# A hand-ordered attention and MoE kernel: other orders for its five engines' instruction lists

## The chip, the cores and the metric

The kernel runs on one core of a Trainium2 chip. The core has five engines with an instruction stream each: TensorE (PE, with its weight loads shown as PEld), VectorE (DVE), ScalarE (ACT), GpSimd (POOL) and SyncE (SP). Each stream runs in order, and an instruction that waits holds back all that stand behind it on its engine. The metric is device microseconds of one execution; less is better. The times are medians of a few runs.

## What is computed

Causal attention over 8 batches of 8 heads (576 tokens of 64 values, 16 extra "beacon" keys and values that every token sees), then a two-layer MLP with a quick GELU on the 4608 tokens that come out:

```python
k_all = np.concatenate([beacon_k, k], axis=2)
v_all = np.concatenate([beacon_v, v], axis=2)
scores = scale * np.matmul(q, k_all.transpose(0, 1, 3, 2))
scores = np.where(causal, -1000000000.0, scores)
a = np.exp(scores - scores.max(-1, keepdims=True))
a /= a.sum(-1, keepdims=True) + 1e-09
x = np.matmul(a, v_all)            # (8, 8, 576, 64), then 4608 tokens x 512
h = x @ w_in                       # 512 -> 2048
g = h * (1.0 / (1.0 + np.exp(-1.702 * h)))
out = g @ w_out                    # 2048 -> 512
```

## The kernel before

**Tiling.** Attention is done in 16 sets: a set is four heads of one batch (`HS = 2` sets a batch). For each set, queries and keys are loaded by GpSimd's DMA queue (`e_load_qk`, L397), transposed on DVE (`e_turn`, L446, with the line of the transposes at L455), and multiplied on TensorE in chunks of at most 512 score columns a head (`e_qk`, L474; four row tiles of 32). The chunks are numbered through: qk0 to qk54. ACT takes the exponential of each chunk from PSUM (`e_exp`, L492). POOL, and DVE for the first two sets, put zeros in the masked corners (`e_mask`, L502). Then `e_av` (L565; column tiles of 32) multiplies with the values, or with ones for the sum of each row; DVE makes the reciprocal of the sums (`e_z1`, `e_z2`) and writes the product to the activations `xT` (`e_norm`). A visit named av5.0.1 is set 5, part 0, half 1.

The tokens go through the MLP in ten groups: two of 256 tokens, then eight of 512. m1.1.4 is the first layer (`e_m1`, L619) of group 1 for hidden tile 4. Groups 0 and 1 apply the activation as a tanh on ACT (`e_tanh`, L640) and a gate on DVE (`e_gate`, L660, its instruction at L663), the later ones as one gelu on ACT. m2.0.1.2 is the second layer of group 0, row half 1, third quarter of the hidden rows (`e_m2`). Groups 2 to 9 use Strassen-like products of 2x2 blocks for the second layer (`e_prod`, named m2.g.p.n) with joins on DVE, and groups 7 to 9 also for the first (`e_part`).

**What sets the order.** The kernel schedules by hand. Every step is recorded as an operation with a number, an engine, a price and the operations it depends on (`Plan.op`). The table `ORDER` lists, for each engine, the numbers in the order in which it issues them; "Q" lists the landings of POOL's loads, which are no instructions. `Plan.run` (L150) replays these lists with the prices, which gives each operation a planned start, and the steps are then written out in the order of planned starts (L1320). The replay also picks the PSUM bank for each visit that needs one: the bank that is free first. Four banks serve all visits but qk while attention runs; the scores of qk take the other four.

**Names that matter below.** Numbers in the lists: 129, 131, 134 are qk5, qk6, qk7; 152, 161, 158, 164, 167, 170, 173 are m1.0.0, m1.0.6, m1.0.4, m1.0.8, m1.0.10, m1.0.12, m1.0.14, and the number behind each of these is its tanh on ACT (165 for m1.0.8), the next one its gate on DVE. 188, 191, 194, 197, 203, 200 are m1.1.0, m1.1.2, m1.1.4, m1.1.6, m1.1.10, m1.1.8; their gates are 190, 193, 196, 199, 205, 202. On POOL, 53 and 55 load the keys and the queries of set 3, 57 and 59 the third and the fourth quarter of the second layer's weights w2 (`e_load_w2`, L426, 512 KB of 16-bit values each), 133, 137 and 136 are masks of set 1. On DVE, 255 casts set 3's beacon keys, 256 transposes its keys (a small transpose of the beacon keys is part of it) and 257 its queries. POOL has eight completion semaphores for loads; each load waits for the landing of the eighth before it. The first layer's weights w1 come in four column blocks, each in two loads (upper and lower half of the rows); m1.0.6 needs the second block.

Of the kernel before, what the change touches and what calls it, by code (L numbers as in the profile page):

```python
# [17 lines left out]
        76, 100, 115, 118, 120, 106, 138, 141, 143, 108, 155, 111, 152, 129, 161, 158, 122, 131, 164, 167, 134, 127,  # L18
        170, 173, 176, 145, 125, 148, 150, 177, 182, 188, 191, 227, 194, 197, 232, 183, 203, 234, 200, 178, 237, 179,
        206, 258, 241, 209, 184, 263, 185, 212, 265, 213, 248, 246, 268, 214, 215, 401, 251, 253, 272, 218, 404, 275,  # L20
        244, 279, 219, 220, 407, 282, 284, 277, 221, 414, 320, 296, 304, 290, 302, 292, 300, 298, 312, 308, 294, 318,
        314, 310, 306, 316, 426, 435, 423, 343, 338, 339, 340, 433, 431, 438, 344, 345, 359, 349, 341, 464, 346, 350,
        351, 352, 354, 574, 355, 429, 360, 361, 577, 356, 362, 357, 372, 365, 583, 474, 477, 373, 366, 374, 367, 605,
        480, 484, 375, 482, 607, 368, 506, 502, 488, 492, 610, 490, 486, 498, 504, 500, 508, 514, 510, 516, 494, 496,
        512, 534, 593, 596, 535, 536, 539, 540, 550, 541, 542, 537, 742, 545, 546, 547, 548, 603, 745, 551, 552, 553,
        599, 601, 619, 622, 748, 555, 556, 557, 558, 561, 755, 625, 627, 629, 562, 563, 776, 568, 564, 569, 570, 571,
        779, 764, 767, 659, 637, 641, 657, 649, 651, 647, 661, 635, 631, 653, 805, 772, 770, 774, 643, 655, 633, 639,
        645, 679, 680, 815, 818, 700, 681, 682, 684, 701, 915, 690, 685, 686, 691, 692, 702, 918, 687, 693, 695, 703,
        696, 924, 821, 823, 697, 698, 706, 946, 825, 707, 713, 708, 709, 948, 934, 937, 714, 715, 716, 827, 951, 944,
        940, 942, 853, 831, 833, 855, 857, 851, 843, 835, 837, 847, 839, 845, 829, 849, 841, 1083, 960, 963, 875,  # L30
        876, 880, 877, 878, 881, 882, 1086, 968, 966, 970, 883, 1089, 902, 909, 903, 886, 891, 1096, 887, 888, 889,
        892, 893, 1117, 904, 894, 905, 896, 897, 1120, 898, 899, 910, 911, 1105, 1108, 1146, 912, 976, 994, 996, 972,
        978, 1000, 1002, 992, 984, 990, 986, 988, 974, 980, 982, 998, 1168, 1111, 1115, 1159, 1113, 1156, 1025, 1026,
        1020, 1027, 1171, 1021, 1022, 1028, 1023, 1031, 1177, 1032, 1033, 1164, 1166, 1162, 1199, 1034, 1036, 1047,
        1048, 1037, 1201, 1041, 1042, 1038, 1039, 1233, 1049, 1204, 1043, 1044, 1050, 1235, 1237, 1054, 1055, 1056,
        1057, 1239, 1249, 1190, 1241, 1265, 1251, 1242, 1253, 1255, 1187, 1245, 1267, 1258, 1281, 1257, 1269, 1216,
        1195, 1197, 1193, 1213, 1261, 1271, 1285, 1287, 1283, 1273, 1289, 1274, 1219, 1221, 1223, 1334, 1290, 1293,
        1277, 1357, 1335, 1313, 1318, 1314, 1336, 1315, 1319, 1316, 1320, 1321, 1373, 1324, 1325, 1337, 1326, 1329,
# [9 lines left out]
        1, 3, 77, 79, 103, 101, 107, 109, 112, 153, 156, 130, 159, 162, 132, 165, 168, 135, 171, 174, 189, 192, 228,  # L48
        195, 198, 233, 235, 201, 204, 238, 180, 207, 259, 210, 264, 186, 266, 269, 216, 402, 405, 408, 222, 417, 415,
        297, 291, 303, 305, 301, 299, 293, 309, 321, 295, 319, 313, 315, 311, 307, 317, 436, 439, 342, 465, 468, 575,  # L50
        578, 584, 587, 606, 608, 503, 507, 489, 491, 493, 487, 499, 505, 509, 515, 517, 495, 501, 511, 497, 513, 611,
        538, 743, 746, 749, 756, 758, 777, 780, 660, 642, 638, 652, 658, 648, 650, 636, 632, 662, 654, 806, 644, 634,
        656, 640, 646, 809, 916, 683, 919, 928, 925, 947, 949, 952, 828, 832, 854, 856, 852, 858, 834, 838, 844, 840,
        836, 846, 830, 848, 850, 842, 1084, 879, 1087, 1090, 1099, 1097, 1118, 1121, 1147, 1150, 977, 995, 997, 973,
        979, 1001, 993, 985, 991, 989, 1003, 975, 981, 987, 983, 999, 1169, 1172, 1024, 1181, 1178, 1200, 1202, 1234,
        1205, 1236, 1238, 1240, 1250, 1252, 1244, 1266, 1254, 1256, 1268, 1248, 1246, 1264, 1270, 1260, 1282, 1262,
        1272, 1286, 1284, 1288, 1276, 1280, 1292, 1294, 1296, 1278, 1358, 1317, 1374, 1378, 1376, 1360, 1362, 1364,
# [5 lines left out]
        73, 74, 75, 97, 98, 99, 80, 81, 82, 78, 116, 105, 87, 104, 117, 102, 121, 119, 139, 140, 144, 142, 157, 154,  # L63
        123, 163, 160, 124, 224, 169, 128, 166, 172, 175, 146, 147, 126, 149, 151, 225, 226, 398, 190, 193, 196, 199,
        255, 256, 257, 202, 205, 286, 242, 411, 287, 211, 208, 243, 399, 249, 247, 400, 250, 412, 254, 252, 273, 245,
        274, 280, 276, 413, 281, 285, 283, 278, 289, 461, 288, 462, 419, 580, 420, 463, 326, 327, 328, 421, 322, 92,
        323, 324, 422, 427, 428, 424, 425, 325, 330, 334, 329, 335, 432, 336, 331, 434, 337, 332, 333, 470, 347, 582,
        353, 471, 581, 472, 430, 473, 358, 363, 475, 476, 478, 479, 481, 485, 739, 483, 369, 376, 370, 589, 752, 740,
        590, 615, 518, 753, 921, 519, 754, 526, 591, 527, 520, 528, 592, 529, 521, 741, 522, 597, 523, 594, 530, 595,
        598, 531, 802, 532, 524, 533, 616, 543, 525, 604, 549, 617, 618, 554, 600, 620, 602, 623, 624, 621, 559, 760,  # L70
        628, 761, 762, 626, 630, 565, 763, 566, 768, 572, 765, 811, 812, 766, 803, 804, 769, 773, 771, 671, 1080,
        775, 672, 813, 922, 663, 814, 664, 675, 667, 816, 673, 819, 668, 669, 817, 923, 665, 666, 820, 674, 676, 677,
        1093, 670, 688, 694, 678, 930, 822, 824, 699, 931, 826, 932, 933, 704, 710, 938, 939, 935, 936, 717, 711,
        945, 941, 943, 1081, 956, 957, 958, 871, 1082, 1094, 1095, 959, 872, 873, 1225, 867, 859, 961, 962, 964, 965,
        860, 863, 1174, 1143, 861, 874, 862, 868, 864, 967, 865, 971, 866, 969, 884, 869, 870, 1101, 1144, 890, 1145,
        1102, 895, 1226, 1103, 1104, 900, 906, 1109, 907, 1110, 913, 1106, 1107, 1152, 1153, 1227, 1176, 1175, 1154,
        1012, 1004, 1005, 1155, 1006, 1112, 1116, 1008, 1160, 1016, 1013, 1009, 1157, 1161, 1007, 1114, 1158, 1017,
        1010, 1011, 1014, 1029, 1018, 1183, 1165, 1163, 1019, 1229, 1015, 1230, 1035, 1228, 1231, 1167, 1184, 1040,
        1232, 1209, 1045, 1185, 1051, 1052, 1186, 1058, 1210, 1191, 1243, 1192, 1247, 1211, 1212, 1188, 1189, 1263,
        1259, 1217, 1196, 1198, 1194, 1214, 1215, 1297, 1218, 1275, 1291, 1220, 1279, 1295, 1298, 1222, 1301, 1302,  # L80
        1303, 1305, 1309, 1306, 1310, 1353, 1299, 1354, 1307, 1322, 1300, 1355, 1356, 1224, 1308, 1311, 1304, 1312,
# [3 lines left out]
        1557, 1555, 1558, 1559, 1546, 1547, 1551, 1560, 1552, 1570, 1548, 1556, 1576, 1581, 1592, 1586, 1593, 1599,  # L85
    ],
    "POOL": [
        8, 10, 12, 14, 16, 17, 19, 21, 23, 25, 27, 29, 31, 33, 35, 37, 39, 41, 43, 45, 47, 110, 49, 51, 113, 114, 53,
        55, 57, 59, 133, 61, 136, 137, 63, 65, 67, 69, 71, 378, 230, 231, 229, 380, 382, 384, 386, 236, 388, 390,
        392, 239, 240, 394, 396, 261, 260, 262, 441, 443, 270, 267, 271, 449, 451, 453, 455, 457, 459, 403, 406, 445,  # L90
        447, 416, 409, 410, 437, 418, 719, 721, 466, 467, 440, 585, 588, 579, 576, 586, 469, 727, 723, 725, 729, 731,
        733, 735, 737, 609, 782, 784, 612, 613, 614, 747, 751, 744, 750, 757, 790, 792, 794, 786, 788, 796, 798, 800,
        778, 759, 781, 1060, 1062, 807, 808, 917, 920, 926, 810, 927, 1068, 1070, 1072, 1074, 1066, 1064, 1076, 1078,
        954, 955, 929, 950, 953, 1125, 1123, 1088, 1085, 1131, 1133, 1135, 1137, 1139, 1141, 1091, 1129, 1127, 1098,
        1092, 1122, 1100, 1149, 1119, 1151, 1148, 1170, 1179, 1173, 1180, 1203, 1206, 1208, 1182, 1207,
    ],
    "Q": [
# [1260 lines left out]
```

## Time and profile before

| | us |
|---|---|
| median of 3 runs (lowest to highest) | 324.79 (324.67 to 325.13) |
| the profiled execution: its own time | 324.84 |
| its span, first to last instruction | 323.1 |
| mean granted TensorE clock | 0.992 |
| first qk visit starts | 8.27 |
| ACT: idle time ended by a qk visit | 40.9 in 38 waits |
| POOL: idle time ended by an exponential | 94.2 in 16 waits |
| PE: idle time ended by an exponential | 2.0 in 4 waits |
| DMA: POOL's loads, packets and volume | 47,552, 18.49 MB |

Busy time is the time in which an engine's instructions run, idle time the gap before an instruction, put down to what ended it. TensorE's matmuls overlap in the pipeline, so that a matmul of 256 columns is shown as 273 ns though the next starts 109 ns later: steps from start to start say what TensorE is worth, durations do not. A load's own time is short on POOL (some 0.55 us for queries or keys, 0.75 us for a quarter of w2); its landing is a mark of its own, microseconds later.

### The profile page before, as it was taken

How to read it: one execution, taken by the hardware profiler on the slowest of the kernel's cores; microseconds unless marked ns; L12 is line 12 of the kernel's file. 1: busy time of each engine (PE TensorE's matmuls, PEld its weight loads, DVE VectorE, ACT ScalarE, POOL GpSimd, SP SyncE). 2: the span in 40 equal slices, each digit the busy share in tenths (PEclk: the TensorE clock that was granted, in tenths of full speed). 3: DMA queues.
4: the chain of work that ended last, by engine and by line, in shares of the span. 5: the costliest groups of instructions: out<-in, count | busy, mean ns of one | idle time of the engine just before them, and what ended most of it. 6: DMA issues, size and time to landing. Idle time of an engine off the chain costs nothing. (4 is left out here: it accounts for less than half of the span.)

```text
span 323.1 us, 10371 instructions
## 1 busy us (share of the span) xinstructions
PE 312.2 (97%) x4508; PEld 230.0 (71%) x4508; DVE 261.7 (81%) x524; ACT 219.5 (68%) x272; POOL 113.4 (35%) x178
## 2 busy tenths in 40 slices
PE   7689999999999999999999999999999999999994
PEld 7467665644776467745878877646888888888884
DVE  4837798777987989976998889986999895585784
ACT  1676597677767686689767696768778735974830
POOL 8775478190328403871058208600221000000000
PEclk9899999999999999999999999999999999999998
DMA  7999999294423941396019908900111001101112
GB/s 124 163 200 208 206 185 184 54 97 85 123 70 66 185 73 34 53 183 89 2 36 134 189 3 80 176 28 2 37 34 65 4 32 34 67 2 36 65 67 97
DMA packets 58222, 28.85 MB, mean 89 GB/s; under 512 B 41280, under 2 KB 53568, under 8 KB 58176
## 3 DMA queue, kind: packets, MB, share of 16 engines
q0 software_dynamic: 47552, 18.49, 48.4%
q1 hardware_dynamic: 10560, 9.69, 9.3%
q8 instruction: 35, 0.57, 0.7%
q14 instruction: 11, 0.09, 0.1%
q10 hardware_dynamic: 64, 0.01, 0.0%
HBM read 37.22 MB, written 9.44 MB: 144 GB/s over the span
## 5 line engine op out<-in xcount | busy, mean ns | idle before, releaser
L495 ACT ACTIVATE E<-s 128x2048 f16<-128x2048 f32 (+5 forms) x66 | 98.9, 1515 | 41.4 <-PE s L484 40.9
L630 PE MATMUL u<-xT,w 128*128 128x256 f16 (+1 forms) x512 | 87.3, 326 | 0.6 <-ACT g L651 0.5
L516 POOL TENSOR_SCALAR_AFFINE_SELECT E<-E 128x512 f16<-128x512 f16 (+3 forms) x78 | 48.8, 658 | 107.5 <-ACT E L495 94.2
L630 PEld LDWEIGHTS <-w 128*128 128x128 f16 x512 | 49.0, 98 | 34.7 <-issue 1.9
L651 ACT ACTIVATE g<-u 128x512 f16<-128x512 f32 x80 | 43.2, 599 | 15.6 <-PE u L630 15.4
L744 PEld LDWEIGHTS <-g 128*128 128x128 f16 x512 | 48.5, 98 | 7.1 <-issue 0.3
L744 PE MATMUL u<-w,g 128*128 128x256 f16 x384 | 49.9, 273 | 0.0
L760 DVE SCALAR_TENSOR_TENSOR osb<-u,osb 128x512 f32<-128x512 f32 x56 | 37.6, 683 | 13.6 <-PE u L744 11.7
L484 PEld LDWEIGHTS <-kT 32*128 32x128 f16 x1376 | 25.6, 93 | 20.6 <-issue 12.1
L744 PEld LDWEIGHTS <-sA 128*128 128x128 f16 x384 | 36.3, 98 | 5.1 <-issue 0.3
L484 PE MATMUL s<-qT,kT 32*128 32x32 f16 (+20 forms) x1376 | 34.9, 230 | 3.9 <-ACT E L495 2.0
L859 ACT ACTIVATE g<-u 128x512 f16<-128x512 f32 x48 | 26.9, 602 | 12.4 <-PE u L831 6.8
L744 PE MATMUL u<-tB,sA 128*128 128x256 f16 x256 | 34.9, 273 | 0.1
L606 DVE TENSOR_TENSOR xT<-u,rz 128x352 f16<-128x352 f32 (+2 forms) x52 | 25.8, 518 | 7.4 <-PE u L571 7.1
L415 POOL DMA_DIRECT2D vb<-in_v_dram x32 | 27.4, 876 | 2.2 <-DMA qn<-in_q_dram 1.2
L571 PE MATMUL u<-E,vb 128*32 128x352 f16 (+8 forms) x928 | 27.9, 265 | 0.0
L534 DVE TENSOR_TENSOR zs<-zs,E 128x1344 f16<-128x1344 f16 (+2 forms) x36 | 22.6, 628 | 2.3 <-POOL E L516 1.6
L571 PEld LDWEIGHTS <-vb 128*32 128x32 f16 (+1 forms) x928 | 19.8, 97 | 5.5 <-issue 1.5
L455 DVE STREAM_TRANSPOSE kT<-kn 128x576 f32<-128x576 f32 x16 | 20.1, 1258 | 2.3 <-DMA kn<-in_k_dram 1.5
L831 PE MATMUL u<-xT,w 128*128 128x256 f16 x144 | 20.5, 273 | 0.0
L831 PEld LDWEIGHTS <-w 128*128 128x128 f16 x192 | 18.8, 98 | 2.2
L455 DVE STREAM_TRANSPOSE qT<-qn 128x576 f32<-128x576 f32 x16 | 19.9, 1241 | 0.1
(73 smaller groups left out, 397.5 us busy)
## 6 DMA issues: line engine op xcount, KB each, us to landing
out_dram<-osb SPq DMA_DIRECT2D x36, 256.0 KB, 2.3
kn<-in_k_dram POOLq DMA_DIRECT2D x16, 288.0 KB, 6.3
qn<-in_q_dram POOLq DMA_DIRECT2D x16, 288.0 KB, 6.8
vb<-in_v_dram POOLq DMA_DIRECT2D x24, 128.0 KB, 6.6
w<-in_moe_w_in_dram POOLq DMA_DIRECT2D x8, 256.0 KB, 9.6
w<-in_moe_w_out_dram POOLq DMA_DIRECT2D x4, 512.0 KB, 13.8
vb<-in_v_dram POOLq DMA_DIRECT2D x8, 112.0 KB, 5.0
vb<-in_v_dram POOLq DMA_DIRECT2D x8, 80.0 KB, 7.8
```

The costliest lines, as they stand in the source:

```text
L415: nc.gpsimd.dma_start(out=t[0 : hi - lo, j, h0:h1, :], in_=v[b, h0:h1, lo:hi, :].rearrange("h n d -> n h d"),)
L455: nc.vector.transpose(out=f32(dst.rearrange("p n e -> p (n e)")).rearrange("p (r t) -> p t r", t=TR), in_=f32(src[:, :]).rearrange("p (t c ...
L484: nc.tensor.matmul(sc[:, h, o : o + w], kT[s % NB2][r : r + 32, j * P : (j + 1) * P, d], qT[s % NB2][r : r + 32, a : a + w, d], start=(d = ...
L495: nc.scalar.activation(out=Es[s][:, :, c0:c1], in_=ss[i][:, :, o : o + c1 - c0], func=AFT.Exp, scale=0.125,)
L516: nc.gpsimd.affine_select(out=blk, in_=blk, compare_op=ALU.is_ge, fill=0.0, base=off + (Nb if j == 0 else 0), pattern=[[0, Q], [1, w]], ch ...
L571: nc.tensor.matmul(u[32 * h : 32 * h + 32, a:e], lhs, src[0:kw, h, col : col + e - a], start=first, stop=last,)
L630: nc.tensor.matmul(u[:, o + a - t0 : o + e - t0], w1t[:, kp, nt * P : (nt + 1) * P], xT[:, kp, a % XR : (e - 1) % XR + 1], start=(kp == 0) ...
L651: nc.scalar.activation(out=gts[g][:, n0:n1, 0:w], in_=rings[("m1", g, n0)][:, 0 : n * w].rearrange("p (n w) -> p n w", n=n), func=AFT.Gelu ...
L744: nc.tensor.matmul(u[:, HM * mt : HM * (mt + 1)], lhs[:, n, mt * P : (mt + 1) * P], rhs[:, n, :], start=(n == 0 and mt == 0), stop=(n == H ...
L760: nc.vector.scalar_tensor_tensor(out=osbs[(g, dst)][:, :], in0=rings[("p", g, p)][:, :], scalar=scale_of(g), in1=osbs[(g, src)][:, :], op0 ...
L831: nc.tensor.matmul(u[:, HM * n : HM * (n + 1)], lhs[x][:, (2 * i + n) * P : (2 * i + n + 1) * P], rhs[:, x, :], start=fresh and n == 0 and ...
L859: nc.scalar.activation(out=gts[g][:, n : n + 2, HM * h : HM * (h + 1)], in_=rings[src][:, :].rearrange("p (n w) -> p n w", n=2), func=AFT. ...
```

## The change

Only the lists in `ORDER` differ. No operation is added or taken away: each engine has the same numbers, 559 on PE, 260 on ACT, 465 on DVE, 171 on POOL. PE's list differs from its 14th place to its 432nd, ACT's from its 15th to its 203rd, DVE's from its 23rd to its 385th, POOL's from its 27th to its last. The lists of SP and Q are the same. Because the planned starts follow from the lists, visits also get other PSUM banks.

The beginning of each changed list:

```diff
     "PE": [
-        76, 100, 115, 118, 120, 106, 138, 141, 143, 108, 155, 111, 152, 129, 161, 158, 122, 131, 164, 167, 134, 127,
-        170, 173, 176, 145, 125, 148, 150, 177, 182, 188, 191, 227, 194, 197, 232, 183, 203, 234, 200, 178, 237, 179,
...
+        76, 100, 115, 118, 120, 106, 138, 141, 143, 108, 155, 111, 152, 161, 129, 158, 164, 131, 167, 170, 134, 122,
+        173, 176, 125, 127, 145, 150, 148, 182, 177, 188, 191, 227, 183, 194, 197, 232, 184, 203, 234, 200, 178, 237,
...
     "ACT": [
-        1, 3, 77, 79, 103, 101, 107, 109, 112, 153, 156, 130, 159, 162, 132, 165, 168, 135, 171, 174, 189, 192, 228,
...
+        1, 3, 77, 79, 103, 101, 107, 109, 112, 153, 156, 130, 159, 162, 165, 132, 168, 171, 135, 174, 189, 192, 228,
...
     "DVE": [
...
-        123, 163, 160, 124, 224, 169, 128, 166, 172, 175, 146, 147, 126, 149, 151, 225, 226, 398, 190, 193, 196, 199,
-        255, 256, 257, 202, 205, 286, 242, 411, 287, 211, 208, 243, 399, 249, 247, 400, 250, 412, 254, 252, 273, 245,
...
+        163, 160, 224, 166, 169, 172, 123, 124, 175, 255, 126, 128, 146, 147, 149, 151, 225, 226, 190, 193, 257, 256,
+        196, 199, 202, 286, 398, 205, 208, 242, 399, 211, 461, 243, 400, 413, 247, 249, 245, 411, 273, 250, 274, 254,
...
     "POOL": [
-        8, 10, 12, 14, 16, 17, 19, 21, 23, 25, 27, 29, 31, 33, 35, 37, 39, 41, 43, 45, 47, 110, 49, 51, 113, 114, 53,
-        55, 57, 59, 133, 61, 136, 137, 63, 65, 67, 69, 71, 378, 230, 231, 229, 380, 382, 384, 386, 236, 388, 390,
...
+        8, 10, 12, 14, 16, 17, 19, 21, 23, 25, 27, 29, 31, 33, 35, 37, 39, 41, 43, 45, 47, 110, 49, 51, 113, 114,
+        133, 53, 137, 136, 57, 55, 59, 65, 61, 69, 71, 63, 67, 378, 229, 231, 384, 380, 230, 390, 239, 382, 394, 396,
```

In the built program the same change on POOL reads, in instructions (a line with L516 is a mask, L399 a load of queries or keys, L428 a quarter of w2):

```diff
 L399 DMACopy qn_93<-in_q_dram 128x1152
 L516 TensorScalarAffineSelect E<-E 128x4x128
+L516 TensorScalarAffineSelect E<-E 128x4x80 x2
+L399 DMACopy kn_94<-in_k_dram 128x1152
 L516 TensorScalarAffineSelect E<-E 128x4x80
-L399 DMACopy kn_94<-in_k_dram 128x1152
+L516 TensorScalarAffineSelect E<-E 128x4x128
+L428 DMACopy w_81<-in_moe_w_out_dram 128x4x512
 L399 DMACopy qn_91<-in_q_dram 128x1152
-L428 DMACopy w_81<-in_moe_w_out_dram 128x4x512 x2
...
+L428 DMACopy w_81<-in_moe_w_out_dram 128x4x512
```

Set 3's queries are the load into `qn_91`; its keys go to `kn_94`.

## The prediction

> **What bounds the kernel now.** I read part 1 of the page first, then the busy time of each engine by stretches of 20 us, then the order of time on PE, DVE and POOL in the first 45 us.
>
> ```profile
> PE 312.2 (97%) x4508; PEld 230.0 (71%) x4508; DVE 261.7 (81%) x524; ACT 219.5 (68%) x272; POOL 113.4 (35%) x178
> ...
> 0.00:20.00 20.00, 14.86 (x291) 12.79 (x292) 12.17 (x33) 8.59 (x8) 16.15 (x30) 0.91 1.25 154
> 20.00:40.00 20.00, 19.11 (x347) 14.05 (x345) 13.51 (x27) 13.56 (x18) 10.54 (x17) 1.00 1.20 207
> 40.00:60.00 20.00, 19.95 (x398) 12.17 (x400) 17.17 (x29) 16.47 (x16) 14.02 (x24) 1.00 1.55 174
> ...
> 180.00:200.00 20.00, 20.00 (x295) 16.44 (x293) 18.60 (x40) 15.24 (x19) 5.01 (x7) 1.00 0.45 69
> ```
>
> The columns of the stretches are length, then busy us of PE, PEld, DVE, ACT, POOL, then clock, DMA share and GB/s. From 40 us on PE has no hole to speak of. The DMA share is over 1 in the first 60 us: there the loads are the scarce thing. Busy PE is not PE at its peak, so I took each TensorE visit's usual length from the starts of its matmuls (start of a visit to start of the next, lower quartile of its like) and added them in order: 302.6 us of pure work. I call a visit's start less the work ahead of it its lag. Before, the lag is 8.27 at qk0 (only filler ran earlier), 12.62 at m1.0.4 (22.52 us), 12.97 at qk8 (36.24), 13.20 at m1.1.10 (40.22), 13.53 at qk19 (64.88) and 16.16 at the last visit (318.46): only about 2.6 us of waits are left after 65 us. A reorder can win little there; it can lose anywhere.
>
> ```profile
> 23.65 0.55 POOL L399 DMA_DIRECT2D kn<-in_k_dram  x1
> 24.48 0.53 POOL L399 DMA_DIRECT2D qn<-in_q_dram  x1 [0.28 <-issue]
> 25.49 0.75 POOL L428 DMA_DIRECT2D w<-in_moe_w_out_dram  x1 [0.48 <-DMA w<-in_moe_w_in_dram]
> 26.77 0.75 POOL L428 DMA_DIRECT2D w<-in_moe_w_out_dram  x1 [0.53 <-DMA w<-in_moe_w_in_dram]
> ...
> 36.98 0.69 DVE L663 SCALAR_TENSOR_TENSOR g<-sig,u 128x512 f16<-128x512 f16 x1 [0.19 <-ACT sig L644]
> 39.35 1.28 DVE L663 SCALAR_TENSOR_TENSOR g<-sig,u 128x512 f16<-128x512 f16 x2 [1.68 <-ACT sig L644]
> 40.55 1.33 DVE L440 CAST bkn<-bkf 128x64 f16<-128x64 f32 x1
> 41.92 0.21 DVE L448 STREAM_TRANSPOSE kT<-bkn 128x32 f32<-128x32 f32 x1
> 42.17 1.26 DVE L455 STREAM_TRANSPOSE kT<-kn 128x576 f32<-128x576 f32 x1
> 43.27 1.23 DVE L455 STREAM_TRANSPOSE qT<-qn 128x576 f32<-128x576 f32 x1
> ...
> 40.22 1.04 PE L630 MATMUL u<-xT,w 128*128 128x256 f16 x8
> ```
>
> POOL issues set 3's keys, then its queries, then the last two quarters of w2. By the tile views of these issues they land 12.2, 12.7, 14.2 and 15.8 us later: at 35.8, 37.2, 39.7 and 42.6. Set 3's transposes (L455) stand behind four gates (L663) of group 1.
>
> **The change, part by part.**
>
> *Fewer changes of TensorE's tiling.* Counted in the lists, changes between full-array, row-tiled (qk) and column-tiled (av) visits go from 150 to 144. A 256-column full-array step takes 0.109 us to the next start, 0.205 where a tiled visit follows; the last 80-wide step of an av takes 0.030 before another av and 0.133 before anything else. So 0.1 us each, 6 x 0.1; with each kind of change at its own price, -0.59. Nothing else of the pure work moves: 302.05.
>
> *m1.0.6 ahead of qk5.* Before, PE waits 0.61 us at 20.98 for qk4's exp, runs qk5, then m1.0.6 at 21.45, whose third matmul stands from 21.57 to 21.85. Its weights (second w1 load, lower half, issued at 11.54) land 10.3 us later, at 21.81. After, m1.0.6 starts at 20.20 and its third matmul waits to 21.85 all the same, with qk5 now queued behind it: qk5 at 22.61 instead of 20.98, m1.0.4 at 23.08 instead of 22.52. Lag +0.56.
>
> *m1.0.8's tanh ahead of qk6's exp on ACT.* qk5's exp starts at 23.23 and occupies 1.35; three tanhs of 0.48 follow (24.58 to 26.02), then qk6's exp ends at 27.47. qk7 waits for it to 27.52, where PE would be there at 27.24: +0.28 (lag 13.46).
>
> *What disappears.* av1.2.1 stood 0.34 for set 1's masks (POOL ends them at 30.97; it started at 30.22). After it starts at 31.5 and they end near 31.0. qk9 stood 0.19 for qk8's exp; a product visit is put between. So at qk8 and until m1.1.10 the lag is 13.53 against 13.20. Set 2's transposes end near 36.55 and qk8 comes at 36.7: no wait.
>
> *The loads of set 3 and the DVE list (the main term).* POOL now takes: set 1's mask (L516), set 3's keys, two masks, w2 third quarter, set 3's queries, w2 last quarter. The masks need set 1's last exp (28.35 to 29.8), so these issues come at 28.1, 31.0, 31.7 and 32.3. That alone costs nothing: the queue is busy with earlier loads until 34.6 (set 2's queries land then). But the queries go in behind a w2 quarter, and all 42 loads that landed in the first 57 us did so in the order of issue. A w2 quarter takes 39.73 - 37.21 = 2.52 us of the queue. So the queries land at 39.7, not 37.2. On DVE the transposes of set 3 are moved ahead of the gates of m1.1.4 and m1.1.6, queries first. DVE runs in order: queries 39.78 (next start 1.08 later), keys with the small transpose to 42.2 (1.35), gate of m1.1.4 to 42.9. m1.1.10 takes m1.1.4's PSUM bank (two banks are held by the unfinished output of group 0, so only two serve m1), and PE is there at 13.53 + 27.78 = 41.31. It starts at 42.98: +1.67, lag 15.2. Behind it qk10 and all of PE wait. This price is hidden nowhere: later loads are not what PE waits for. Bounds: 0.1 if the queries land at 37.2 as before (transposes from 38.2, gate to 41.3); 2.2 if the queue also runs dry for 0.5 us because w2's quarter is issued 5.5 us later.
>
> The Trainium skill (DMA: Bandwidth & Descriptors, section Two DMAs through the same engine are not ordered) says that descriptors of a queue start in order, but that completion isn't promised in order and that nothing orders DMAs across the 16 engines. By that, the queries could overtake the quarter, and the end would come up to 1.6 us earlier. The trace disagrees as far as it goes, 42 of 42 in order. It is the first rival.
>
> *To 65 us.* The small waits before had between 40 and 65 us (13.53 - 13.20 = 0.33) fall away, since their exps and loads are then earlier against PE: qk19 comes at 15.2 + 51.26 = 66.5.
>
> *After 65 us.* 0.65 us at m1.2 (fifth visit of group 2, which needs the first gelu behind a table load) stays: the same four visits stand ahead of it. The other 2.0 (visits of products and av waiting a little on a join, an exp or a mask, one or two tenths at a time) depend on order. Comparing each visit's position with the exp, join or norm that it needs, I find spots of 0.1 to 0.2 us in both orders and no load that comes late for its transpose. I carry this at 0, between -1.0 (half of it gone) and +1.1 (the second rival). Stores: SP's list is the same; group 0's second half is copied out first, so its store waits behind the other's, with four output buffers, which holds nobody.
>
> Sum: +0.56 + 0.28 - 0.34 - 0.19 + 0.02 (rounding of the visits between) + 1.67 - 0.33 = +1.67, which is the lag of 15.2 less 13.53 at qk19; less the 0.59 of tiling changes, +1.08. The profiled execution took 324.84 us (span 323.1), so 325.9; the median of the runs is 324.79, the same within 0.05.
>
> **Rivals.**
> 1. *The queries are not late* (they overtake the quarter, or DVE gets to them later than I think). Then the 1.67 is 0.1 at most and the fewer tiling changes and vanished waits show: 325.9 - 1.6 = 324.3, not slower. For it: 0.59 + 0.53 us of real savings. Against: the order of landings. It decides when the queries land before 38.3.
> 2. *DVE bounds the dense part.* DVE is busy 18.6 of 20 us there. In the new order two joins (0.6 each) and a cast stand before the norm that m1.3.8 needs: 0.2 us to spare if the cast takes 0.15, 0.6 late if it takes the 0.95 that the cast at 105.51 took while POOL was issuing loads. With two bank waits of 0.13 and 0.12 (av6.0.1 behind a join, av8.2.0 behind a norm) and one more such cast: +1.1, 327.0.
> 3. *The dense part wins.* Half of the 2.0 us of order-bound waits doesn't come back and the first rival holds as well: 323.3. Against: slacks of both orders look alike.
>
> **How the numbers follow.** Main case 0.60, at 325.9, own range 325.2 to 326.6. Rival 1 0.20 (324.0 to 324.8), rival 2 0.13, rival 3 0.07. A measurement tells about 0.2% (0.65 us) from no change: faster is under 324.1, slower over 325.4. Slower: 0.85 of the main case and rival 2, 0.64. Same: the rest of the main case and two thirds of rival 1, 0.22. Faster: 0.14. The range takes in rival 1's forecast and rival 2's: 324.2 to 327.2.
>
> **What would show it.** Set 3's queries (qn, issued near 31.7) landing near 39.7, behind the w2 quarter; DVE idle from about 38.2 until then; PE standing about 1.7 us before an m1 visit of group 1 near 41.3, released by a gate; m1.0.6's third matmul again at 21.85 with qk5 behind it at 22.6. Wrong if PE has no hole between 36 and 45 us, or if new holes over 1 us in all stand after 80 us.

## The result, and the profile after

The changed kernel takes 329.3 us (median of 4 runs, 329.03 to 329.77) against 324.76 (4 runs, 324.67 to 325.13): ratio 1.0139, 95% interval 1.0122 to 1.0157. It is slower, as forecast, but by 4.5 us where 1.1 was forecast. Its profiled execution took 329.32 us (span 327.6).

Part 1 of the page of the changed kernel, and then busy time by stretches of 20 us (length, busy us of PE, PEld, DVE, ACT, POOL, clock, DMA share, GB/s), first of the changed kernel, then, for the stretches that the prediction doesn't show, of the kernel before:

```profile
PE 313.0 (96%) x4508; PEld 229.8 (70%) x4508; DVE 261.5 (80%) x524; ACT 219.8 (67%) x272; POOL 114.1 (35%) x178
```

```profile
40.00:60.00 20.00, 18.55 (x369) 11.45 (x368) 14.00 (x23) 15.53 (x16) 13.01 (x23) 1.00 1.41 153
...
120.00:140.00 20.00, 19.60 (x377) 15.07 (x376) 18.87 (x43) 12.89 (x10) 10.17 (x17) 1.00 0.40 60
...
160.00:180.00 20.00, 18.94 (x374) 15.24 (x373) 18.67 (x35) 13.04 (x10) 12.83 (x18) 1.00 0.89 125
...
240.00:260.00 20.00, 19.15 (x264) 15.82 (x263) 18.65 (x38) 15.78 (x24) 3.41 (x5) 1.00 0.12 41
```

```profile
120.00:140.00 20.00, 20.00 (x373) 14.57 (x372) 18.28 (x37) 13.80 (x10) 12.34 (x18) 1.00 0.37 55
...
160.00:180.00 20.00, 20.00 (x385) 16.22 (x384) 18.10 (x34) 13.34 (x12) 13.62 (x20) 1.00 0.65 95
...
240.00:260.00 20.00, 20.00 (x291) 16.59 (x289) 18.55 (x39) 16.91 (x30) 2.26 (x4) 1.00 0.12 41
```

The work is the same (no engine's busy time moved by more than 0.8 us); PE has new holes in all four of these stretches. The first, 40 to 60 us (19.95 busy before), is the one forecast. POOL, DVE and PE in order of time there:

```profile
27.61 0.55 POOL L399 DMA_DIRECT2D kn<-in_k_dram  x1
...
30.54 0.77 POOL L428 DMA_DIRECT2D w<-in_moe_w_out_dram  x1
31.31 0.54 POOL L399 DMA_DIRECT2D qn<-in_q_dram  x1
```

```profile
36.52 1.37 DVE L663 SCALAR_TENSOR_TENSOR g<-sig,u 128x512 f16<-128x512 f16 x2
39.83 1.26 DVE L455 STREAM_TRANSPOSE qT<-qn 128x576 f32<-128x576 f32 x1 [1.93 <-DMA qn<-in_q_dram]
40.93 0.18 DVE L448 STREAM_TRANSPOSE kT<-bkn 128x32 f32<-128x32 f32 x1
41.15 1.25 DVE L455 STREAM_TRANSPOSE kT<-kn 128x576 f32<-128x576 f32 x1
42.24 1.27 DVE L663 SCALAR_TENSOR_TENSOR g<-sig,u 128x512 f16<-128x512 f16 x2
```

```profile
40.49 1.04 PE L675 MATMUL u<-w,g 128*128 128x512 f16 x4
42.97 1.03 PE L630 MATMUL u<-xT,w 128*128 128x256 f16 x8 [1.45 <-DVE g L663]
```

DVE idles until set 3's queries land, transposes queries and keys, and only then does the gate that frees m1.1.10's bank. The three later stretches were not forecast. What PE waited for by the profile's list of waits (us in total, times, longest), in the changed kernel and then, the whole list, before:

```profile
PE s L484 <- DVE qT L455: 3.3, 3, 2.3
PE u L571 <- DVE osb L760: 2.0, 4, 1.1
...
PE u L630 <- DVE g L663: 1.4, 1, 1.4
```

```profile
PE s L484 <- ACT E L495: 2.0, 4, 0.9
PE u L1326 <- DVE tB L311: 1.9, 1, 1.9
PE s L484 <- DVE qT L455: 1.6, 2, 1.4
PE u L630 <- ACT g L651: 0.5, 1, 0.5
PE u L571 <- DVE E L509: 0.2, 1, 0.2
```

The changed kernel's second row, av visits that wait for a bank which a join (L760) reads out, has no counterpart before. The lag (a visit's start less the TensorE work ahead of it, as in the prediction) shows where the time went. The first column is the lag at the first visit after 80 us, the others are what it grew by in each stretch:

| | at 80 us | 80–100 | 100–130 | 130–150 | 150–180 | 180–240 | 240–end | sum from 80 us |
|---|---|---|---|---|---|---|---|---|
| before | 14.19 | 0.58 | 0.18 | 0.22 | 0.16 | 0.63 | 0.20 | 1.97 |
| after | 16.03 | 0.60 | 0.74 | 0.49 | 1.45 | 0.48 | 1.46 | 5.22 |

At the last visit the lag is 21.25 against 16.16. 324.84 + 5.09 - 0.59 (fewer tiling changes) = 329.34, which closes on the profiled 329.32. The lag at qk19 (66.71 us) is 15.45; from there on it grew by 5.80, and before by 2.63 (13.53 to 16.16): 3.17 us lie behind 65 us, in eight waits of 0.22 to 1.23 us at av5.2.0 (0.46), av6.0.1 (0.46), av8.2.0 (0.27), av10.2.1 (1.23), m1.6.1 (0.23), f7.0.1 (0.22), av14.2.0 (0.43) and f7.0.7 (0.60), less some 0.7 of waits that the kernel before has there and this one has not.

### The profile page after: what moved, and what is told of

Its sections match the earlier page's. It is cut to its first block, busy times and chain, and to the rows that moved or that the text cites. A ratio compares the mean times of both kernels' runs of the same rounds, so it can differ in the third digit from the quotient of the medians.

```text
span 327.6 us, 10365 instructions
## 1 busy us (share of the span) xinstructions
PE 313.0 (96%) x4508; PEld 229.8 (70%) x4508; DVE 261.5 (80%) x524; ACT 219.8 (67%) x272; POOL 114.1 (35%) x178
## 5 line engine op out<-in xcount | busy, mean ns | idle before, releaser
L516 POOL TENSOR_SCALAR_AFFINE_SELECT E<-E 128x512 f16<-128x512 f16 (+3 forms) x78 | 49.5, 657 | 108.5 <-ACT E L495 94.0
L630 PEld LDWEIGHTS <-w 128*128 128x128 f16 x512 | 49.1, 98 | 37.3 <-issue 3.6
L744 PE MATMUL u<-w,g 128*128 128x256 f16 x384 | 50.6, 273 | 0.0
L760 DVE SCALAR_TENSOR_TENSOR osb<-u,osb 128x512 f32<-128x512 f32 x56 | 37.7, 683 | 12.6 <-PE u L744 10.9
L534 DVE TENSOR_TENSOR zs<-zs,E 128x1344 f16<-128x1344 f16 (+2 forms) x36 | 23.4, 651 | 4.4 <-POOL E L516 3.3
L571 PEld LDWEIGHTS <-vb 128*32 128x32 f16 (+1 forms) x928 | 20.5, 98 | 5.5 <-issue 1.5
L841 ACT ACTIVATE u<-u 128x512 f32<-128x512 f32 x24 | 14.3, 598 | 10.6 <-DVE osb L760 6.3
```

The costliest lines, as they stand in the source:

```text
L516: nc.gpsimd.affine_select(out=blk, in_=blk, compare_op=ALU.is_ge, fill=0.0, base=off + (Nb if j == 0 else 0), pattern=[[0, Q], [1, w]], ch ...
L571: nc.tensor.matmul(u[32 * h : 32 * h + 32, a:e], lhs, src[0:kw, h, col : col + e - a], start=first, stop=last,)
L630: nc.tensor.matmul(u[:, o + a - t0 : o + e - t0], w1t[:, kp, nt * P : (nt + 1) * P], xT[:, kp, a % XR : (e - 1) % XR + 1], start=(kp == 0) ...
L744: nc.tensor.matmul(u[:, HM * mt : HM * (mt + 1)], lhs[:, n, mt * P : (mt + 1) * P], rhs[:, n, :], start=(n == 0 and mt == 0), stop=(n == H ...
L760: nc.vector.scalar_tensor_tensor(out=osbs[(g, dst)][:, :], in0=rings[("p", g, p)][:, :], scalar=scale_of(g), in1=osbs[(g, src)][:, :], op0 ...
```

## The experiments

The first question was whether the early term is what the prediction took it for, and whether the late 3 us belong to the late order or follow from the late start.

**Set 3's queries first.** One number moved in POOL's list:

```diff
-    137, 136, 57, 55, 59,
+    137, 136, 55, 57, 59,
```

> The changed kernel with one load moved on POOL: set 3's queries are issued ahead of the third quarter of w2 instead of behind it. Theory (the queries' place is the main term): they land near 37.2 us, DVE's transposes are through before 41.4, m1.1.10 starts near 41.4 instead of 42.97 and nearly all of its 1.62 us stays gained: 327.7 (327.4 to 328.1). Rival (the gain is swallowed by the later waits, whose instants are set by DVE and POOL rather than by PE): 329.0 to 329.4.

Measured: 327.9 us (6 runs, 327.54 to 328.91), 1.0096 of the kernel before (1.0077 to 1.0115). In its profile m1.1.10 starts at 41.22 without a wait, and the lag is 13.49 at 50 us (15.21 in the changed kernel). The waits behind it are the same eight, each with its size to 0.02 us, 1.8 us earlier. So the main early term is real, and the late waits neither swallow a gain nor grow with the delay.

**Gates first.** The other half of the same mechanism, on DVE; the load stays late:

```diff
-    193, 257, 256, 196, 199, 202,
+    193, 196, 199, 257, 256, 202,
```

> The changed kernel with one edit in DVE's list: the transposes of set 3 (257, 256) behind the gates 196 and 199 instead of ahead of them; the load stays where the change put it and lands near 39.7. Theory (the 1.62 us at m1.1.10 takes both the late load and the transposes' place ahead of the gates; set 3's own first visit, qk12, comes only near 47 and can wait for transposes that end near 44): the wait goes and the end comes at 327.7 (327.3 to 328.2). Rival (the late load alone costs it, qk12 or the loads behind wait instead): 329.0 to 329.5.

Measured: 327.66 us (4 runs, 327.5 to 328.3), ratio 1.0091 (1.0072 to 1.0110). DVE and then PE in order of time:

```profile
39.69 0.69 DVE L663 SCALAR_TENSOR_TENSOR g<-sig,u 128x512 f16<-128x512 f16 x1 [1.99 <-ACT sig L644]
40.56 0.69 DVE L663 SCALAR_TENSOR_TENSOR g<-sig,u 128x512 f16<-128x512 f16 x1 [0.19 <-ACT sig L644]
41.16 1.25 DVE L455 STREAM_TRANSPOSE qT<-qn 128x576 f32<-128x576 f32 x1
```

```profile
41.16 1.04 PE L630 MATMUL u<-xT,w 128*128 128x256 f16 x8
```

The late load alone costs nothing at m1.1.10 and the transposes' place alone costs nothing there; together they cost 1.6 us. Either edit takes the whole wait away.

**Before to 45 us, after behind.** Lists joined where both orders have issued the same set: PE 52 places, ACT 37, DVE 52, POOL 40.

> The lists of the kernel before up to about 45 us, those of the changed kernel behind. At 45 us the lag of the changed kernel was 15.19 against 13.20 before. Theory (the order of the dense part itself costs some 3.4 us, whatever stands ahead of it): 329.3 - 2.0 = 327.3 (326.9 to 327.8). Rival (the later waits are the late start's own consequence and go with it): 324.4 to 325.4.

Measured: 328.06 us (6 runs, 327.03 to 328.57), ratio 1.0092 (1.0073 to 1.0112): above the forecast, though the rival falls. (The kernel before took 325.10 us beside it; 1.0092 of 324.76 would be 327.75, inside the forecast.) From 80 us on the lag grows by 5.27 (5.22 in the changed kernel), with the same waits. The rest is ahead of 45 us: at 40 us this execution (328.57 us, the slowest of the six) had a lag of 14.20, where the kernel before, with the same lists to there, had 13.20.

**After to 45 us, before behind.**

> The reverse: the changed kernel's lists up to about 45 us, those of the kernel before behind. Theory: the early part alone, 324.8 + 2.0 = 326.8, less some 0.3 of small waits that a later PE no longer meets: 326.3 to 326.9. Rival (a late start alone makes the dense part stumble): 328 to 329.5.

Measured: 329.23 us (4 runs, 328.75 to 329.84), ratio 1.0133 (1.0112 to 1.0155). The time is the rival's, the reason is not: between 40 and 80 us the lag grows by 4.47 (14.32 to 18.79). Of this 1.20 is the early lists' own wait at m1.1.10; most of the rest stands at the seam, in waits at av2.2.0 (0.77), qk14 (0.50) and qk16 (1.04), presumably because the lists behind it expect other work to be done already. From 80 us on it grows by 1.96, against 1.97 in the kernel before, though PE is there 4.6 us later. A late start doesn't make the dense part stumble; its own order does.

So the causes had to be sought wait by wait. Candidates: DVE's list (T1: joins behind the additions that make a set's row sums, zadd, L534, which nobody waits for yet), POOL's list (T2: masks behind load issues), PE's list (T4: visits pulled forward), and as a rival to each the amount of DVE work itself.

**Joins ahead on DVE.**

```diff
-    471, 472, 473, 353, 358, 363,
+    471, 472, 353, 358, 363, 473,
...
-    616, 617, 618, 543, 549,
+    616, 617, 543, 549, 618,
...
-    760, 761, 762, 763, 630,
+    630, 760, 761, 762, 763,
...
-    1183, 1184, 1035, 1185, 1231, 1040, 1045, 1186, 1232,
+    1035, 1231, 1232, 1183, 1040, 1045, 1184, 1185, 1186,
```

> The changed kernel with DVE's list changed at four places: joins 353, 358, 363 ahead of the last zadd of set 5, joins 543 and 549 ahead of the last zadd of set 7, the last norm of set 7 ahead of the zadds of set 8, and joins 1035, 1040, 1045 with the two sums 1231 and 1232 ahead of the zadds of set 14. Theory (T1: PE waits for banks that joins release, and the joins stand in DVE's list behind additions nobody waits for): of the 0.46 + 0.46 + 0.27 + 0.22 + 0.43 + 0.60 us of waits at av5.2.0, av6.0.1, av8.2.0, f7.0.1, av14.2.0 and f7.0.7 some 1.2 to 2.0 goes: 327.3 to 328.1. Rival (DVE's amount of work bounds there, the order does not: what is put off is waited for later): 329.0 to 329.6.

Measured: 329.75 us (5 runs, 329.3 to 331.64), ratio 1.0150 (1.0127 to 1.0173): in sum the rival. But the profile splits the sum. (That execution, 331.64 us, lost 1.9 us ahead of 50 us, where its lists are those of the changed kernel; only what lies behind 80 us is read.) PE in the changed kernel at set 5, and then in this one:

```profile
97.36 0.23 PE L571 MATMUL u<-zs,ones 128*32 128x112 f16 x4 [0.29 <-DVE osb L760]
```

```profile
100.27 0.38 PE L571 MATMUL u<-zs,ones 128*32 128x352 f16 x8 [1.21 <-DVE zs L534]
```

Here the edit made it worse: the same visits need the last addition as well as the join's bank, and DVE, with no hole over 0.13 us from 84 to 98 us in the changed kernel, can only exchange one for the other. At set 8 it is the same (0.27 becomes 0.67). At av6.0.1 the wait is gone from the profile, though the visits around it (av7.2.0 to qk31) still lose 0.28 of the 0.46, spread over them; at f7 and set 14 the lag grew by 0.55 instead of 1.46. Two places gained some 1.1 us, two lost as much.

**Masks ahead on POOL.**

```diff
-    920, 1064, 1123, 927, 926, 810,
+    920, 927, 926, 1064, 1123, 810,
```

> The changed kernel with one edit in POOL's list: two masks of set 10 (927, 926) stand ahead of the two load issues 1064 and 1123 instead of behind them. Theory (T2: masks queued behind load issues make the additions late): their exponential ends at 167.43, so they end near 168.7 instead of 169.59, DVE's hole of 0.95 us ahead of the third addition of set 10 goes, and av10.2.1 waits some 0.3 instead of 1.23: 329.3 - 0.9 = 328.4 (328.1 to 328.7). Rival (T4: PE's visit simply stands too early for DVE, whatever POOL does): 329.1 to 329.5.

Measured: 328.27 us (4 runs, 327.84 to 328.8), ratio 1.0104 (1.0085 to 1.0123), the time that T2 forecast. DVE, POOL and PE in the changed kernel:

```profile
167.52 1.16 DVE L534 TENSOR_TENSOR zs<-zs,E 128x1344 f16<-128x1344 f16 x1
169.63 1.84 DVE L534 TENSOR_TENSOR zs<-zs,E 128x832 f16<-128x832 f16 x2 [0.95 <-POOL E L516]
171.38 1.47 DVE L760 SCALAR_TENSOR_TENSOR osb<-u,osb 128x512 f32<-128x512 f32 x2
```

```profile
167.32 1.12 POOL L399 DMA_DIRECT2D kn<-in_k_dram  x2
168.45 2.21 POOL L516 TENSOR_SCALAR_AFFINE_SELECT E<-E 128x320 f16<-128x320 f16 x4
```

```profile
172.12 0.33 PE L571 MATMUL u<-zs,ones 128*32 128x352 f16 x4 [1.06 <-DVE osb L760]
```

and DVE and PE with the masks ahead:

```profile
169.14 1.21 DVE L534 TENSOR_TENSOR zs<-zs,E 128x832 f16<-128x832 f16 x2 [0.53 <-POOL E L516]
170.28 1.46 DVE L760 SCALAR_TENSOR_TENSOR osb<-u,osb 128x512 f32<-128x512 f32 x2
```

```profile
171.01 0.33 PE L571 MATMUL u<-zs,ones 128*32 128x352 f16 x4
```

Two load issues of 0.56 us each, for sets 13 and 14, stand ahead of two masks; the addition behind the masks holds back two joins on DVE; the first join holds PE's bank. av10.2.1 waits 0.19 instead of 1.23, and every wait behind it keeps its size. But the queue is only a part of it: T2 expected DVE's hole ahead of the third addition (0.95) to go, and it went to 0.53. The first join ends 1.10 us earlier (170.96 for 172.06) because the third addition starts 0.49 earlier and takes 0.59 instead of 1.48, less 0.26 by which the fourth is longer; in the changed kernel two more masks ran beside the third addition, and now they stand behind the loads. Both parts were made on an engine that is busy 35% of the time.

**Visits back on PE.** Ahead of the next two runs, the list positions were put side by side in another way: work ahead in its own engine's list, not time (durations: for DVE the shorter of the two profiles).

| PE visit that waits | PE work ahead, before / after | its releaser on DVE | DVE work to its end, before / after |
|---|---|---|---|
| av5.2.0 | 81.7 / 80.8 | join 358 | 78.8 / 79.0 |
| av8.2.0 | 122.3 / 120.6 | norm 630 | 118.1 / 118.4 |
| av10.2.1 | 154.9 / 152.7 | join 699 | 146.2 / 148.3 |
| av14.2.0 | 227.6 / 223.3 | join 1045 | 218.0 / 217.1 |

PE's list pulls each of these visits forward by 0.9 to 4.3 us of work, while DVE has as much or more to do first in three of the four. The run moved them back (PE's list alone):

```diff
-    474, 477, 583, 374,
+    583, 374, 474, 477,
...
-    622, 601, 599, 619, 748,
+    622, 748, 601, 599, 619,
...
-    764, 767, 779, 571,
+    779, 571, 764, 767,
...
-    937, 934, 948, 706, 707, 708, 709, 716,
+    948, 716, 937, 934, 706, 707, 708, 709,
...
-    1190, 1235, 1237, 1239, 1054, 1055, 1056, 1057,
+    1235, 1237, 1190, 1054, 1055, 1056, 1057, 1239,
```

> The changed kernel with PE's list alone edited: ahead of av5.2.1 and av5.2.0 come qk25 and m2.2.3.4; ahead of av6.0.1 comes qk31; ahead of av8.2.1 and av8.2.0 come qk34 and m2.3.3.6; ahead of av10.2.1 come m2.4.3.6 and qk40; f7.0.2 and f7.0.6 ahead of av14.2.0, the four visits of m2.6.3 ahead of f7.0.7. Each stalled visit thereby comes 0.5 to 1.6 us of PE work later, as it did in the kernel before. DVE's list is untouched. Theory (T4: PE's list has pulled the visits that wait for DVE forward by 1 to 4 us of PE work, past DVE's reach): of the 3.5 us of waits at these places 1.8 to 2.6 goes: 326.7 to 327.5. Rival (DVE's amount of work bounds: PE meets the same wait at the next visit): 328.8 to 329.4.

Measured: 330.54 us (4 runs, 330.29 to 330.68), ratio 1.0171 (1.0157 to 1.0185): worse than either forecast. The five waits themselves shrink or go, but each is followed by new ones. PE at set 5:

```profile
97.28 0.66 PE L484 MATMUL s<-qT,kT 32*128 32x208 f16 x40 [0.15 <-ACT E L495]
...
102.40 0.75 PE L571 MATMUL u<-E,vb 128*32 128x352 f16 x20 [0.16 <-DVE osb L760]
```

qk25, brought ahead, now waits for an exponential (0.22 by the lag), as qk31 does (0.72), and the av visits that come later have their sums read out later (L583), which holds the banks of m1.4.14 (0.61) and m2.6.3.0 (0.62), while av5.0.1 (0.33) and m2.4.5.0 (0.53) now wait for joins. From 80 us on the lag grows by 5.79.

**Visits forward, in the kernel before.** The converse:

```diff
-    583, 474, 477,
+    474, 477, 583,
...
-    570, 571, 779, 764, 767,
+    764, 767, 570, 571, 779,
...
-    713, 708, 709, 948, 934, 937,
+    934, 937, 713, 708, 709, 948,
```

> The kernel before with three pairs of visits pulled forward in PE's list, nothing else: av5.2.1 and av5.2.0 by one visit (0.6 us), av8.2.1 and av8.2.0 by three (1.5), av10.2.1 and av10.2.0 by four (1.9). What they wait for was ready 0.10, 0.47 and 0.38 to 0.82 us ahead of them. Theory T4: new waits of about 0.5, 1.0 and 1.2 us in those places, most of them for good: 324.8 + 2.2 = 327.0 (326.0 to 327.6). Rival (the order on DVE and POOL made the waits, PE's does not matter): 324.5 to 325.3.

Measured: 329.39 us (5 runs, 328.24 to 330.43), ratio 1.0133 (1.0111 to 1.0155). PE in the kernel before, then with the visits forward:

```profile
137.14 0.38 PE L571 MATMUL u<-zs,ones 128*32 128x352 f16 x8
...
170.18 0.38 PE L571 MATMUL u<-zs,ones 128*32 128x352 f16 x8
```

```profile
138.31 0.38 PE L571 MATMUL u<-zs,ones 128*32 128x352 f16 x8 [0.96 <-DVE zs L534]
...
172.51 0.38 PE L571 MATMUL u<-zs,ones 128*32 128x352 f16 x8 [1.06 <-DVE zs L534]
```

The three waits came out at 0.55, 1.04 and 1.14 by the lag, where 0.5, 1.0 and 1.2 were expected; the two shown wait for an addition that they read, not for a bank. The rest of the miss is what the visits displaced: qk26 (+0.30), m1.4.5 (+0.36) and m2.4.3.0 (+0.23) wait for an exponential, a gelu and a join, and 0.7 came ahead of 50 us in the profiled execution. So a few visits pulled forward on PE are enough to cost over 3 us in the kernel before, though moving them back alone doesn't mend the changed one: presumably the other lists have been set to them.

**Three edits together** (queries first, masks ahead, visits back):

> The changed kernel with three edits together: set 3's queries ahead of the w2 quarter, the two masks of set 10 ahead of two load issues, and the stalled visits moved back in PE's list. Theory (the three causes are separate and add up): 329.3 - 1.6 - 0.3 (what the wait at av10.2.1 still is once its visit stands later) - 2.2 = 325.2 (324.6 to 325.9), as fast as the kernel before. Rival (the gains overlap, each wait removed lets PE run into the next): 326.5 to 327.8.

Measured: 328.37 us (4 runs, 328.18 to 328.78), ratio 1.0107 (1.0092 to 1.0122): above the rival's range too, since the third edit costs and does not gain. From 80 us on the lag grows by 5.62.

**The four edits that each gained.** Queries first, masks ahead, and of the joins on DVE only the two places that gained (sets 7 and 14); PE's list is the changed kernel's:

> The changed kernel with four edits: set 3's queries ahead of the w2 quarter and the two masks of set 10 ahead of two load issues on POOL; on DVE joins 543 and 549 ahead of the last zadd of set 7, and join 1035, sums 1231 and 1232, joins 1040 and 1045 ahead of the zadds of set 14. PE's list is that of the changed kernel. Theory (the excess is the sum of separate waits, each with its own place in a list; those at av5.2.0 and av8.2.0 stay): 327.5 (the queries alone) - 1.03 (av10.2.1) - 0.47 (av6.0.1) - 0.93 (f7.0.1 to f7.0.7) = 325.1 (324.7 to 325.7). Rival (waits removed come back further on, as they did when PE's visits were moved back): 326.3 to 327.5.

Measured: 325.65 us (10 runs, 324.96 to 326.13), ratio 1.0023 (1.0012 to 1.0033). PE in the changed kernel at set 14 and f7, and then here:

```profile
243.98 0.23 PE L571 MATMUL u<-zs,ones 128*32 128x112 f16 x4 [0.35 <-DVE osb L760]
...
245.68 0.60 PE L831 MATMUL u<-xT,w 128*128 128x256 f16 x4 [0.43 <-ACT E L495]
```

```profile
240.74 0.23 PE L571 MATMUL u<-zs,ones 128*32 128x112 f16 x4
...
242.60 1.91 PE L744 MATMUL u<-w,sA 128*128 128x256 f16 x16 [0.16 <-DVE zt L583]
```

The wait at f7.0.7 passes through ACT, here in the changed kernel and then with the four edits:

```profile
243.26 0.58 ACT L841 ACTIVATE u<-u 128x512 f32<-128x512 f32 x1 [2.19 <-DVE osb L760]
243.76 1.87 ACT L495 ACTIVATE E<-s 128x2048 f16<-128x2048 f32 x1
```

```profile
239.32 0.58 ACT L841 ACTIVATE u<-u 128x512 f32<-128x512 f32 x1 [0.86 <-PE u L831]
239.92 1.88 ACT L495 ACTIVATE E<-s 128x2048 f16<-128x2048 f32 x1
```

f7.0.7 takes one of the four banks of the scores, which are free when the last exponential ends (245.63; it starts at 245.68). That exponential stands on ACT behind a copy (L841) that waits for the bank of a join, 1040, and the join stands on DVE behind additions of set 14. (The sum that f7.0.7 reads, 1232, had ended at 244.50.) 3.65 of the 4.5 us come back by moving some ten instructions on POOL and DVE. From 80 us on the lag grows by 3.08; av5.2.0 (0.47), av8.2.0 (0.27) and 0.28 around av6.0.1 stay.

**The best of both.** The changed lists with the queries first up to 103 us (PE 138 places, DVE 133, ACT 72, POOL 80), the kernel before's behind:

> The changed kernel's lists, with set 3's queries ahead of the w2 quarter, up to about 103 us (PE place 138, DVE 133, ACT 72, POOL 80), the lists of the kernel before behind. Theory: with the queries in place the lag at 103 us is that of the kernel before within 0.1, five of the tiling changes (0.50 us) are already saved, and the order before costs 1.3 us more to the end as it did: 324.8 - 0.4 = 324.4 (323.9 to 325.0), level with the kernel before or a little under. Rival (two orders do not fit together at a seam, as at 45 us where the seam cost some 2.5 us): 325.8 to 327.5.

Measured: 324.68 us (11 runs, 324.18 to 325.02), ratio 0.9993 (0.9983 to 1.0003). This seam costs nothing. It is level with the kernel before; the 0.5 us of tiling changes that it saves are matched by a lag higher by 0.44 (16.60 against 16.16), half of which is there at 50 us. And with the first two swaps undone in it:

```diff
-    161, 129,
+    129, 161,
...
-    165, 132,
+    132, 165,
```

> The kernel of the run before (the changed lists to 103 us with the queries ahead, the kernel before's behind) with the first two swaps undone: qk5 ahead of m1.0.6 on PE, qk6's exponential ahead of m1.0.8's tanh on ACT. Theory (the prediction's two early terms, +0.56 and +0.28, are real costs): qk7's lag falls from 13.35 towards 12.6, and with the waits that come back for it (0.53 at av1.2.1 and qk9) the end comes 0.3 to 0.8 earlier: 324.1 (323.8 to 324.4). Rival (a later wait, or when the first loads land, sets the lag at qk8 whatever these two do): 324.5 to 324.9.

Measured: 324.83 us (12 runs, 324.3 to 325.94), ratio 1.0001 (0.9993 to 1.0010): no gain to be seen. In its profile qk4 starts at 20.06, 0.7 later than in the run before it, and the lag stays higher from there to qk8 (14.17 against 13.61). Whether the two swaps cost what was forecast stays open: when the first loads land varies more than that. No version run here beats the kernel before by more than a measurement can tell.

## Why the prediction was wrong

**Right: the main term.** Set 3's queries were to land at 39.7 and landed at 39.80, transposed from 39.83; m1.1.10 was to start at 42.98 and started at 42.97; its step was +1.67, measured +1.62. Two runs that take one half of the mechanism away each get 1.4 and 1.6 us back by the medians. The bound of 0.1 for "the queries land as before" was right as well (no wait at all). That the size agrees to 0.05 is luck: in the profiles of the four other versions that keep both halves the same wait was 1.20 (after to 45 us), 1.33 (masks ahead), 1.61 (visits back) and 2.04 us (joins ahead).

**Right in the sum, by luck: the small early terms.** The lag at qk8 was forecast at 13.53 and measured at 13.56, but by other steps. PE in the changed kernel:

```profile
20.31 1.92 PE L630 MATMUL u<-xT,w 128*128 128x256 f16 x16
22.16 0.53 PE L484 MATMUL s<-qT,kT 32*128 32x288 f16 x24
...
36.73 0.64 PE L484 MATMUL s<-qT,kT 32*128 32x288 f16 x24 [0.19 <-DVE qT L455]
```

m1.0.6 ran through without the stop at its third matmul, since its weights landed at 20.48 this time and not at 21.81. So qk5 came at 22.16, not at 22.61, and m1.0.4 at 22.63, not at 23.08: +0.11 instead of +0.56. In its place m1.0.8 stopped for a later w1 load, qk4 had started 1.0 us later than before (19.84 for 18.84), and qk8 waited for set 2's queries by 0.25 where the prediction has "no wait". The stop itself is no invention: in the run of the best of both the third matmul does wait, to 21.71, with the weights landing at 21.67. But executions with the same early lists differ by more than these terms: the lag at 40 us is 13.20 and 14.20 with the lists of before, 13.56 and 14.32 with the changed ones. av1.2.1's wait did go, as forecast; the first two terms, undone together in the last of the runs above, could not be told from the spread.

Rival 1 needed the queries to overtake the w2 quarter. The changed kernel's quarter and queries landed in the order of issue again (38.41 and 39.80 us). The Trainium skill (DMA: Bandwidth & Descriptors, Two DMAs through the same engine are not ordered) promises no such order; no run here shows it broken.

**Nearly right: "To 65 us".** qk19 forecast at 66.5 (lag 15.2), measured at 66.71 (15.45): small waits did not vanish, 0.25.

**Wrong: "After 65 us ... I carry this at 0, between -1.0 and +1.1".** It was +3.17, and with the 0.25 that is the whole miss of 3.4 us (329.32 against 325.9). The prediction's own sign of being wrong, new holes over 1 us in all behind 80 us, is what the profile shows. Rival 2 had the right resource (a DVE that is busy 18.6 of 20 us) with a third of the size: its av6.0.1 measured 0.46 for 0.13, its av8.2.0 0.27 for 0.12, its m1.3.8 (0.6) came to 0.15, and it had none of av5.2.0, av10.2.1, av14.2.0 and f7.0.7, 2.7 us together. The step that failed is how the slack was reckoned: "comparing each visit's position with the exp, join or norm that it needs". That asks when the operands of a join are ready, and leaves out what the join is queued behind on its own engine. (The prediction did follow DVE's queue at m1.1.10 and at m1.3.8, and there it came near.) The table of work ahead shows what moved: three of those four visits are pulled 0.9, 2.2 and 4.3 us forward on PE, while the DVE work ahead of their releasers changed by +0.2, +2.1 and -0.9. But the table was made with the result at hand, and it doesn't pick these visits out: by the same sum m1.3.8 lost more, 4.6 us forward on PE with 2.3 us more on DVE, and waited 0.15. What a visit waits depends on when its releaser's own queue stands still. For the largest, 1.23 at av10.2.1, that is one queue further: mask behind load issue on POOL, addition behind mask on DVE (and slowed from 0.60 to 1.48 us beside other masks), join behind addition, bank behind join. For f7.0.7 it leads from a join through ACT.

The fewer tiling changes (-0.59) were not tried alone; the profiled times close with it to 0.02 us.

What stays open: whether av5.2.0 and av8.2.0 (0.73 together) can be mended at all within the changed order. Moving DVE's list made them longer; moving PE's list took them away and cost more elsewhere. Why a run with set 7's joins ahead still loses 0.28 around av6.0.1 is open too.

## What to carry to other kernels

A reorder of an in-order engine is not judged by dependences alone: for each wait of the bounding engine, follow its releaser down through the queue of each engine on the way, to the first instruction that really waits, and compare the work ahead of both ends. An engine with little to do (POOL here) can hold the longest of these waits, if something that is urgent stands behind something that is not. Waits found so are separate sums when their releaser stands behind work that nobody needs yet, and then moving one instruction wins about its size; where the bounding engine needs both what stands ahead and what stands behind, a swap only changes the wait's name.

## What the runs showed of the hardware

- The same instruction takes longer beside another engine. The 832-wide addition on DVE (L534) took 0.60 us in the kernel before and 1.48 in the changed one, where masks ran on POOL for 1.03 of it; a mask of set 10 (926) took 0.62 in the changed kernel and 1.25 with the masks ahead, beside the 1344-wide addition. The Trainium skill (SBUF — State Buffer, Who interferes with whom) has it that a DVE instruction with two SBUF inputs contends with a GpSimd instruction that reads SBUF, and that the order of issue decides which of the two is held up. The traces agree, in both directions. Over the whole kernel it comes to little, as all additions of L534 are busy 38.5 us after and 38.4 before; at av10.2.1 it stood ahead of PE's bank.
- When the first loads land varies from one execution to the next by more than most terms of the prediction: the weights of m1.0.6 landed at 21.81 us before and at 20.48 in the changed kernel, and qk4 started between 18.40 and 20.06 us in the profiles of kernels that share their lists to there, or nearly so. Part of it is made good by 40 us, where the lag lies between 13.20 and 14.32.
